# Routing of tokens inside an attention kernel: scratch in PSUM, larger groups, scatters at most three a tile, keys' sums on one engine

## The chip, the cores and the metric

The kernel runs on one core of one Trainium2 chip. The core has a matrix engine (TensorE, "PE" in the profile; its weight loads are shown apart as "PEld"), a vector engine (VectorE, "DVE"), a scalar engine (ScalarE, "ACT"), a general engine (GpSimd, "POOL") and the engine that issues most DMA transfers (SyncE, "SP"). SBUF is the on-chip memory of 128 partitions from which the engines read; PSUM is the small memory into which TensorE writes, in banks of 512 float32 for each partition. The metric is device time in microseconds (us) of one execution. A profile's "clock" is the TensorE clock that the throttle granted, as a share of full speed.

## The reference

Attention over pooled keys and values, then a layer of eight experts of which each token uses one, or none:

```python
# q, k, v: (8 batches, 8 heads, 576 positions, 64)
k_p = k.reshape(B, H, 72, 8, D).mean(axis=3)      # 72 pooled keys a head
v_p = v.reshape(B, H, 72, 8, D).mean(axis=3)
scores = scale * q @ k_p.transpose(0, 1, 3, 2)
attn = softmax(scores, axis=-1)                   # denominator + 1e-9
x = (attn @ v_p) as (4608 tokens, 512)

do_compute = x @ w_skip > 0
logits = x @ w_gate                               # 8 experts
e_idx = argmax(logits)
gate = softmax(logits)[e_idx]                     # denominator + 1e-9
out = x
out[do_compute] += gate * (relu(x @ w1[e_idx]) @ w2[e_idx])
```

## The kernel before

**Tiles.** The 4608 tokens are 36 tiles of 128 (`NT = 36`). A batch is four and a half tiles, so some tiles hold halves of two batches. A loop `for t in range(NT)` writes out a software pipeline by hand: in step t, PE computes the scores of tile t (`scores`, two halves), ACT the exponentials of tile t-1 (`exped`), PE the transposes of tile t-2 (`transposed`, `LAG` below is 4), PE the products with the values of tile t-4 (`values`, PSUM tile `o`), and DVE the division of tile t-5 (`normalised`: `rs` L353, `rc` L355, `l` L359, `x` L360, then the transfer of `x` to `out`). There is one `o`, so the products of a tile wait until DVE has read the tile before (L360). DVE also takes the largest score (`nm`, L302), whose result ACT needs. Sums of keys are done in `pool_k`: eight neighbours are added, for batches from 2 on as four additions of halves on POOL (L205, operand `stage`) and then four reductions of four on DVE (L208).

**Values.** `pool_v` adds the eight neighbours of a batch's values on POOL (L229 to L231, reading and writing `hlo`, `hhi` and `vl`; called the chain of a batch below), has PE and ACT work out their products with the skip and gate weights (`gs`), and writes the operand `vbd` of `values` on POOL (L272; the three buffers are vbd_121 to vbd_123 in the listings, used by batches b mod 3). Each output row of `values` thereby holds nine router numbers for each head beside the attention output.

**Routing.** `normalised` sums the nine router numbers over heads into `lg` in SBUF (L363). When a group of tiles is complete (`GROUPS`, here 6, 6, 6, 6, 6, 4 and 2 tiles), `route` is put on a queue of generators: it finds the largest logit (`r_mx`), which tokens skip (`r_no`, L379), the first expert that attains it (`r_eq`, `r_cm`, `r_oh`), by PE the rank of each token among those of its expert (`mps`, L399, read at L400 and L401), the place of the token's row in a table (`r_di`) and the gate (`r_se`, `pay`, L413). Then POOL issues one indirect DMA for each tile of the group (L415), which scatters the pairs of token and gate into `table` in DRAM. The function `extra` gives each step of t a budget (`BUDGET`) of these DVE instructions, after `nm` of the tile; a piece of keys' sums takes its share first, and one `w1lo` (the low part of a split weight, L538, on DVE) may follow. All instructions of one engine run in the order in which the program emits them.

**Early pair.** When the third group (tiles 0 to 17) is routed, `near_tokens` reads back the first expert's first 256 rows of the table (`nids`, L428, an SP transfer, which must wait for the scatters) and, `NWAIT = 3` steps of t later, gathers their rows of `out` by two indirect DMAs on POOL (L445).

**Order of the rest.** Weights of the first expert are loaded, rounded and split from tile 13 on (`w1hi`, `w1lo`, `w2hi`, `w2lo`; the low parts of w2 on POOL, L540). After tile 35 there is a tail until about 227 us, and then the experts' products, which keep PE busy to the end.

Of the kernel before, what the change touches and what calls it, by code (L numbers as in the profile page):

```python
# [26 lines left out]
F32 = mybir.dt.float32  # L27
F32R = mybir.dt.float32r
BF16 = mybir.dt.bfloat16
I32 = mybir.dt.int32  # L30
# [15 lines left out]
VA = HD + 10  # L46
GROUPS = [6, 6, 6, 6, 6, 4, 2]
EARLY = 18
# [12 lines left out]
WPOOL = 3  # L61
BUDGET = 7
DRAIN = 8
# [9 lines left out]
BIT = 3  # L73
NWAIT = 3
WARM = 3
# [83 lines left out]
def attention(tc, nc, q, k, vm, vr, cf, w1, w2, whi, wlo, out, c, pay, offs, table, load_constants, near, bufs, late, early, fin):  # L159
    with ExitStack() as ctx:  # L160
# [17 lines left out]
        for t in vl4:  # L178
            nc.gpsimd.memset(t[64:128], 0.0)
        lg = sp.tile([128, NT, 9], F32, name="lg")  # L180

# [10 lines left out]
        def pool_k(b, kt):  # L192

            kp_ = kp.tile([128, 4, SP], F32, name="kp")
            halves = [slice(hh * 64, hh * 64 + 64) for hh in range(2)]
            if b == 0:
                for g in range(4):
                    nc.vector.tensor_reduce(kp_[:, g], kt[:, g], axis=AX.X, op=ALU.add)
                    for hh, r in enumerate(halves):
                        nc.scalar.activation(kbd[0][r, g, hh * SP:(hh + 1) * SP], kp_[r, g], AF.Copy, scale=-SCALE)  # L200
                return
            n = POOL if b == 1 else 4
            if b > 1:
                for g in range(4):
                    nc.gpsimd.tensor_tensor(kt[:, g, :, 0:4], kt[:, g, :, 0:4], kt[:, g, :, 4:8], ALU.add)  # L205
            yield
            for g in range(4):
                nc.vector.tensor_reduce(kp_[:, g], kt[:, g, :, 0:n], axis=AX.X, op=ALU.add)  # L208
                yield
            for hh, r in enumerate(halves):  # L210
                nc.scalar.activation(kbd[b % 3][r, :, hh * SP:(hh + 1) * SP], kp_[r], AF.Copy, scale=-SCALE)
            yield
# [100 lines left out]
        def transposed(e):  # L313
# [7 lines left out]
            nc.scalar.activation(flat(pT), flat(pt), AF.Copy)  # L321
            pr = ps_p.tile([128, 4, 128], F32, name="pr")

            for a in range(2):
                nc.tensor.transpose(pr[:, a, :], part(a * 4 * SP + 128 - a * 2 * KL), ident)
            nc.scalar.activation(p4, pr[:, 0:2], AF.Copy)
            return pT, p4
# [16 lines left out]
        def normalised(t, os):  # L344
            x = ap.tile([128, H, HD], F32, name="x", bufs=3)
            l8 = ap.tile([128, H, 9], F32, name="l8")
            rs = ap.tile([128, 2, 4], F32, name="rs")
# [14 lines left out]
            yield  # L362
            nc.vector.tensor_reduce(lg[:, t, :], l8.rearrange("p h c -> p c h"), axis=AX.X, op=ALU.add)  # L363
            yield

        scatters = []

        def route(t0, n):

            l = lg[:, t0:t0 + n, 0:NE]  # L370
            skip = lg[:, t0:t0 + n, NE]
            bc = lambda x: x.unsqueeze(2).broadcast_to([128, n, NE])
            new = lambda name, *s, dt=F32: ap.tile([128, GMAX] + list(s), dt, name=name)[:, :n]
            mx = new("r_mx"); eq = new("r_eq", NE); cm = new("r_cm"); oh = new("r_oh", NE, dt=BF16); no = new("r_no")
            d = new("r_d", NE); ex = new("r_ex", NE); se = new("r_se")
            r8 = new("r_r8", NE); ds = new("r_ds"); di = new("r_di", dt=I32)
            nc.vector.tensor_reduce(mx, l, axis=AX.X, op=ALU.max)
            yield
            nc.vector.tensor_scalar(no, skip, 0.0, float(NO_TOKEN), ALU.is_le, ALU.mult)  # L379
            yield  # L380
            nc.vector.tensor_tensor(eq, l, bc(mx), ALU.is_equal)
            yield
            nc.vector.tensor_tensor(d, l, bc(mx), ALU.subtract)
            yield
            nc.vector.tensor_tensor(eq, eq, epos.unsqueeze(1).broadcast_to([128, n, NE]), ALU.mult)
            yield
            nc.vector.tensor_reduce(cm, eq, axis=AX.X, op=ALU.max)
            yield
            nc.vector.tensor_tensor(cm, cm, no, ALU.add)
            yield  # L390
            nc.vector.tensor_tensor(oh, eq, bc(cm), ALU.is_equal)
            yield NEXT
            nc.scalar.activation(ex, d, AF.Exp)

            pr = flat(ps_m.tile([128, 4, 128], F32, name="mps"))[:, 0:(n + 1) * NE].rearrange("p (j e) -> p j e", e=NE)
            for j in range(n):
                nc.tensor.matmul(pr[:, j:], c["ones"], oh[:, j].unsqueeze(1).broadcast_to([128, n + 1 - j, NE]),
                                 start=(j == 0), stop=False)
            nc.tensor.matmul(pr[:, 0:n], c["lower"], oh, start=False, stop=True)  # L399
            nc.vector.tensor_tensor(r8, pr[:, 0:n], offs.unsqueeze(1).broadcast_to([128, n, NE]), ALU.add)  # L400
            nc.vector.tensor_tensor(offs, offs, pr[:, n], ALU.add)  # L401
            yield NEXT
# [5 lines left out]
            yield  # L408
            nc.vector.tensor_scalar(se, se, 1e-9, None, ALU.add)
            yield  # L410
            nc.vector.tensor_tensor(di, ds, no, ALU.add)
            yield
            nc.vector.reciprocal(pay[:, t0:t0 + n, 1], se)  # L413
            for j in range(n):
                m = nc.gpsimd.indirect_dma_start(table, bass.IndirectOffsetOnAxis(ap=di[:, j:j + 1], axis=0),  # L415
                                                 pay[:, t0 + j, :], None, bounds_check=NE * NTOK - 1, oob_is_err=False)
                for other in scatters:
                    tc.declare_no_dep(m.ins, other, reason="rows of the table are written once")
                scatters.append(m.ins)
            if t0 + n == EARLY:  # L420
                yield from near_tokens()

        def near_tokens():
# [3 lines left out]
            nn = ap.tile([128, 1], F32, name="nn")  # L427
            nc.sync.dma_start(near["ids"], table[0:256].rearrange("(s l) t -> l s t", l=128))  # L428
            nc.vector.tensor_scalar(nn, count, 256.0, 2.0, ALU.is_ge, ALU.mult)
# [10 lines left out]
            nc.gpsimd.memset(bufs["ring"], 0.0)  # L440

            def gathers():
                nc.vector.tensor_scalar(near["slot"], near["ids"][:, :, 0], less, None, ALU.add)
                for i in range(2):
                    nc.gpsimd.indirect_dma_start(bufs["ring"][:, 3 + i, 0:D], None, out[0:EARLY * 128],  # L445
                                                 bass.IndirectOffsetOnAxis(ap=near["slot"][:, i:i + 1], axis=0),
                                                 bounds_check=EARLY * 128 - 1, oob_is_err=False)
            later[t + NWAIT] = gathers
            yield
# [145 lines left out]
        def extra(budget):  # L595

            if kcur in kg and t > max(0, 4.5 * kcur - KAHEAD):
                next(kg[kcur], None)
                if kcur == 1:
                    next(kg[kcur], None)  # L600
                budget -= 4
            while budget > 0 and routes.step():
# [4 lines left out]
        def add_routes(n):  # L607
            if n in ends:
                routes.gens.append(route(*ends[n]))

        def sums():
# [4 lines left out]
        for t in range(NT):  # L616
# [59 lines left out]
            if t >= WSTART:  # L676
                next(wgen, None)
            later.pop(t, lambda: None)()
            if t == NT - 4:
# [9 lines left out]
        for i, t in enumerate(range(NT - LAG, NT)):  # L689
# [8 lines left out]
            if i > 0:  # L698
                for _ in range(DRAIN):
                    routes.step(True)  # L700
            while los:
                los.pop(0)[1]()
# [33 lines left out]
        for _ in tail():  # L736
            side(STEP)
        for wait in slots(tc, nc, c, offs, table, near, bufs, out, fin, ap, ps_m):
            if wait:
# [509 lines left out]
```

## Time and profile before

| | before |
|---|---|
| time, median of 3 runs | 577.87 us (578.71, 575.75, 577.87) |
| profiled execution | 576.28 us, of which the span of instructions is 574.5 us |
| mean granted clock | 0.955 |
| attention, tiles 0 to 35 and tail | to about 227 us |
| experts | from there to 574.5 us |

The profile's page lists the busy time of each engine, the chain of work that ended last, and groups of instructions by line. In an entry "L360 x<-o,rc" the line is 360, the output `x` and the inputs `o` and `rc`. A timeline row gives start, duration, engine, line and operation, shape, and in brackets how long the engine had been idle and what released it. A busy time says little here: DVE is busy for half of the span, but PE waits for single instructions of it.

### The profile page before, as it was taken

What the parts mean: (1) busy time and instruction counts of PE and PEld (TensorE: products, weight loads), DVE (VectorE), ACT (ScalarE), POOL (GpSimd) and SP (SyncE); (2) the same over time, 40 slices, a digit from 0 to 9 for tenths busy, and PEclk for the clock granted to TensorE, in tenths of its full rate; (3) what the DMA queues carried; (4) which work ended last, traced back from release to release, by engine and by line L of the source; (5) the groups of instructions that cost most, each with busy time, mean ns of one, the idle gap of its engine ahead of it and who ended that gap; (6) DMA issues with size and microseconds to landing.
All of it is one profiled execution on the core that took longest, in us unless ns stands there. A gap on an engine that the chain in (4) does not pass through costs nothing. (4 is left out here: it accounts for less than half of the span.)

```text
span 574.5 us, 11135 instructions
## 1 busy us (share of the span) xinstructions
PE 518.3 (90%) x3347; PEld 464.5 (81%) x3348; DVE 315.4 (55%) x750; ACT 244.6 (43%) x672; POOL 234.5 (41%) x315
## 2 busy tenths in 40 slices
PE   7589979867499985899999999999999999999994
PEld 4389878767488964888889989989889888989893
DVE  3777886887566762224453535322363638465653
ACT  5458784847478101114142423112243436344441
POOL 4859496848843542311232123323242024304032
PEclk9679997978799998999999999999999999999998
DMA  8948897952579201111551235101144537572300
GB/s 296 395 182 311 299 200 254 262 215 102 204 221 234 96 2 39 48 39 41 200 173 41 81 143 184 63 29 52 55 138 153 188 130 248 191 255 68 124 26 8
DMA packets 33448, 86.05 MB, mean 150 GB/s; under 512 B 7485, under 2 KB 7746, under 8 KB 31488
## 3 DMA queue, kind: packets, MB, share of 16 engines
q1 hardware_dynamic: 25312, 71.62, 38.0%
q0 software_dynamic: 8096, 13.95, 7.4%
q8 instruction: 19, 0.31, 0.3%
q14 instruction: 21, 0.17, 0.1%
HBM read 73.79 MB, written 20.52 MB: 164 GB/s over the span
## 5 line engine op out<-in xcount | busy, mean ns | idle before, releaser
L1046 PE MATMUL psl<-xhi,w1hi 128*128 128x256 f32 (+3 forms) x416 | 122.1, 293 | 5.0 <-PEq L876 4.0
L1048 PE MATMUL psl<-xhi,w1lo 128*128 128x256 f32 (+3 forms) x416 | 121.3, 292 | 0.0
L1047 PE MATMUL psl<-xlo,w1hi 128*128 128x256 f32 (+3 forms) x416 | 121.3, 292 | 0.0
L965 POOL DMA_INDIRECT out<-ring,slot x39 | 39.5, 1013 | 180.2 <-POOLq L876 172.5
L1102 ACT ACTIVATE hhi<-psl 128x256 fp32r<-128x256 f32 (+4 forms) x104 | 41.9, 403 | 156.1 <-ACTq L876 155.1
L1061 PE MATMUL psf<-w2hi,hhi 128*128 128x512 f32 x240 | 96.1, 400 | 2.8 <-PEq L876 2.8
L1062 PE MATMUL psf<-w2lo,hhi 128*128 128x512 f32 x240 | 94.8, 395 | 0.0
L1159 DVE SCALAR_TENSOR_TENSOR hlo<-psl,hhi 128x256 fp32r<-128x256 f32 (+2 forms) x104 | 43.8, 423 | 79.2 <-DVEq L876 79.0
L1046 PEld LDWEIGHTS psl<-xhi,w1hi 128*128 128x128 f32 x416 | 78.1, 188 | 6.9 <-issue 6.3
L1064 PE MATMUL psf<-w2hi,hlo 128*128 128x512 f32 x200 | 79.1, 395 | 0.0
L1047 PEld LDWEIGHTS psl<-xlo,w1hi 128*128 128x128 f32 x416 | 78.2, 188 | 0.5
L1048 PEld LDWEIGHTS psl<-xhi,w1lo 128*128 128x128 f32 x416 | 78.1, 188 | 0.0
L339 PE MATMUL o<-vbd,pT 128*128 128x148 f32 (+1 forms) x304 | 53.8, 318 | 24.7 <-DVE x L360 20.3
L309 ACT ACTIVATE e<-sc,nm 128x72 f32<-128x72 f32 x288 | 64.6, 344 | 21.3 <-DVE nm L302 21.1
L339 PEld LDWEIGHTS o<-vbd,pT 128*128 128x128 f32 (+1 forms) x304 | 44.1, 194 | 27.6 <-issue 20.9
L1148 DVE SCALAR_TENSOR_TENSOR ring<-psf,ring 128x512 f32 x25 | 18.8, 750 | 79.0 <-DVEq L876 79.0
L1061 PEld LDWEIGHTS psf<-w2hi,hhi 128*128 128x128 f32 x240 | 45.1, 188 | 12.9 <-issue 3.2
L1062 PEld LDWEIGHTS psf<-w2lo,hhi 128*128 128x128 f32 x240 | 45.1, 188 | 9.7
L960 POOL DMA_INDIRECT ring<-out,slot x39 | 43.6, 1119 | 14.9 <-issue 12.5
L1111 ACT ACTIVATE xhi<-psd 128x512 fp32r<-128x512 f32 x36 | 18.9, 600 | 70.9 <-ACTq L876 70.9
L415 POOL DMA_INDIRECT table<-pay,r_di x36 | 36.4, 1010 | 30.9 <-DVE rc L355 11.5
L1064 PEld LDWEIGHTS psf<-w2hi,hlo 128*128 128x128 f32 x200 | 37.6, 188 | 9.1
(207 smaller groups left out, 914.6 us busy)
## 6 DMA issues: line engine op xcount, KB each, us to landing
stage<-in_w SPq DMA_DIRECT2D x64, 512.0 KB, 4.4
out<-x SPq DMA_DIRECT2D x36, 256.0 KB, 4.9
stage<-in_k SPq DMA_DIRECT2D x7, 1152.0 KB, 10.1
hlo<-in_vm SPq DMA_DIRECT2D x4, 1024.0 KB, 8.2
hhi<-in_vm SPq DMA_DIRECT2D x4, 1024.0 KB, 7.3
xlo<-in_q SPq DMA_DIRECT2D x6, 512.0 KB, 7.2
qt<-in_q SPq DMA_DIRECT2D x6, 512.0 KB, 5.6
xhi<-in_q SPq DMA_DIRECT2D x5, 512.0 KB, 7.6
```

The costliest lines, as they stand in the source:

```text
L309: nc.scalar.activation(e[:, h, :], sc[h // 4][:, h % 4 * SP:(h % 4 + 1) * SP], AF.Exp, bias=nm[:, h:h + 1], scale=-1.0)
L339: nc.tensor.matmul(o_[sl, g * 2 * VA:(g + 1) * 2 * VA], pT[:, 2 * a + g, sl], vbd[b % 3][:, 2 * a + g, :], start=(g == 0), stop=False)
L960: g.indirect_dma_start(ring[:, s % 6, 0:D], None, out, bass.IndirectOffsetOnAxis(ap=slot[:, s:s + 1], axis=0), bounds_check=NTOK - 1, oob_ ...
L965: g.indirect_dma_start(out, bass.IndirectOffsetOnAxis(ap=offsets, axis=0), ring[:, s % 6, 0:D], None, bounds_check=NTOK - 1, oob_is_err=Fa ...
L1046: t.matmul(ps, whi[0][:, k, w], xhi[:, k, xs], start=(k == 0), stop=False)
L1047: t.matmul(ps, whi[0][:, k, w], xlo[:, k, xs], start=False, stop=False)
L1048: last = t.matmul(ps, wlo[0][:, k, w], xhi[:, k, xs], start=False, stop=(k == 3))
L1061: t.matmul(ps, hhi[:, k, sl], whi[1][:, k, :], start=(k == 0), stop=False)
L1062: last = t.matmul(ps, hhi[:, k, sl], wlo[1][:, k, :], start=False, stop=(short and k == 7))
L1064: last = t.matmul(ps, hlo[:, k, sl], whi[1][:, k, :], start=False, stop=(k == 7))
L1102: a.activation(hhi[:, f, xs], psL[f % 3][:, xs], AF.Relu).then_inc(sem["act"], 1)
L1159: m = v.scalar_tensor_tensor(to[:, f], psL[f % 3][:, cs], 0.0, hhi[:, f, cs].bitcast(F32), ALU.max, ALU.subtract)
```

## The change

Five things are changed.

1. **Scratch in PSUM.** `lg` is gone. The router numbers `l8` of a whole group are kept in SBUF, and the first instruction of `route` reduces them over heads into a piece of PSUM, `scratch`, which is the unused second half of the bank of `pr`, one of the transposes' outputs. The comparisons, differences, ranks and sums of `route` are written there too, with new names in SBUF (`r_cn`, `r_sn`) where needed, so that each DVE instruction of `route` but the last group's has at most one operand in SBUF among its inputs. `r_eq` and its product with `epos` become one instruction (L392), and `r_d` takes the logits' own place. The last group uses a piece of SBUF instead.
2. **Groups** of 9, 9, 7, 6, 3 and 2 tiles, and a larger budget (10, of which a piece of keys' sums takes 7).
3. **Scatters** are not emitted with the gate but put on a list, of which each step of t emits at most three.
4. **Keys' sums** are on DVE alone, one reduction of eight for each of the four pieces.
5. **Early pair:** `nids` is emitted four steps after routing, and the gathers five steps after it.

```diff
-GROUPS = [6, 6, 6, 6, 6, 4, 2]
+GROUPS = [9, 9, 7, 6, 3, 2]
-BUDGET = 7
+BUDGET = 10
-NWAIT = 3
+SCATTERS = 3
+NIDS = 4
+NWAIT = 5
...
-        lg = sp.tile([128, NT, 9], F32, name="lg")
+        l8s = {}
+
+        side_ps = ps_p.tile([128, 4, 128], F32, name="pr")
+        pr, scratch = side_ps[:, 0:2], flat(side_ps)[:, 256:512]
...
-            n = POOL if b == 1 else 4
-            if b > 1:
-                for g in range(4):
-                    nc.gpsimd.tensor_tensor(kt[:, g, :, 0:4], kt[:, g, :, 0:4], kt[:, g, :, 4:8], ALU.add)
             yield
             for g in range(4):
-                nc.vector.tensor_reduce(kp_[:, g], kt[:, g, :, 0:n], axis=AX.X, op=ALU.add)
+                nc.vector.tensor_reduce(kp_[:, g], kt[:, g], axis=AX.X, op=ALU.add)
...
-            pr = ps_p.tile([128, 4, 128], F32, name="pr")
...
-            nc.vector.tensor_reduce(lg[:, t, :], l8.rearrange("p h c -> p c h"), axis=AX.X, op=ALU.add)
...
-            l = lg[:, t0:t0 + n, 0:NE]
-            skip = lg[:, t0:t0 + n, NE]
+            last = t0 + n == NT
+            m = n if last else GMAX
+            room = ap.tile([128, n * 20], F32, name="r_room", bufs=1) if last else scratch
+            lp = room[:, 0:n * 9].rearrange("p (j e) -> p j e", e=9)
+            l, skip = lp[:, :, 0:NE], lp[:, :, NE]
+            r8 = eq = room[:, m * 9:m * 9 + n * NE].rearrange("p (j e) -> p j e", e=NE)
+            cm, se, ds = (room[:, m * (17 + i):m * (17 + i) + n] for i in range(3))
...
+            nc.vector.tensor_reduce(lp, l8s.pop(t0)[:, :n].rearrange("p j h c -> p j c h"), axis=AX.X, op=ALU.add)
...
-            nc.vector.tensor_tensor(eq, l, bc(mx), ALU.is_equal)
-            yield
-            nc.vector.tensor_tensor(d, l, bc(mx), ALU.subtract)
-            yield
-            nc.vector.tensor_tensor(eq, eq, epos.unsqueeze(1).broadcast_to([128, n, NE]), ALU.mult)
+            nc.vector.tensor_tensor(l, l, bc(mx), ALU.subtract)
+            yield
+            nc.vector.scalar_tensor_tensor(eq, l, 0.0, epos.unsqueeze(1).broadcast_to([128, n, NE]), ALU.is_equal, ALU.mult)
...
-            for j in range(n):
+
+            def scatter(j):
                 m = nc.gpsimd.indirect_dma_start(table, ...)
...
+            pending.extend(lambda j=j: scatter(j) for j in range(n))
...
-            nc.sync.dma_start(near["ids"], table[0:256].rearrange("(s l) t -> l s t", l=128))
...
+            def ids():
+                assert not pending
+                nc.sync.dma_start(near["ids"], table[0:256].rearrange("(s l) t -> l s t", l=128))
...
+            later[t + NIDS] = ids
             later[t + NWAIT] = gathers
...
-                budget -= 4
+                budget -= 7
...
         def add_routes(n):
             if n in ends:
+                assert not routes.gens
                 routes.gens.append(route(*ends[n]))
+                next(routes.gens[0])
...
+            for _ in range(min(SCATTERS, len(pending))):
+                pending.pop(0)()
             later.pop(t, lambda: None)()
```

On DVE, at tile 22, the routing of the third group began before the change in the middle of the attention's own work:

```order
L302 TENSOR_REDUCE nm<-sc 128x4 x2
L363 TENSOR_REDUCE lg<-l_1545 128x9
L208 TENSOR_REDUCE kp<-stage 128x72
L377 TENSOR_REDUCE r_mx<-lg 128x6
L379 TENSOR_SCALAR r_no<-lg 128x6
L381 TENSOR_TENSOR r_eq<-lg,r_mx 128x48
L353 TENSOR_SCALAR rs<-o 128x8
L383 TENSOR_TENSOR r_d<-lg,r_mx 128x48
L355 RECIPROCAL rc<-rs 128x8
L385 TENSOR_TENSOR r_eq<-r_eq,cfs 128x48
L359 TENSOR_TENSOR l_1612<-o,rc 128x72
L360 TENSOR_TENSOR x<-o,rc 128x512
```

At the same tile it is now the second group, of nine tiles. In this listing `pr` is the scratch in PSUM, and `cfs` holds the constants (`epos`):

```order
L303 TENSOR_REDUCE nm<-sc 128x4 x2
L384 TENSOR_REDUCE pr<-l_905 128x81
L209 TENSOR_REDUCE kp<-stage 128x72
L386 TENSOR_REDUCE r_mx<-pr 128x9
L388 TENSOR_SCALAR r_no<-pr 128x9
L390 TENSOR_TENSOR pr<-pr,r_mx 128x9x8
L356 TENSOR_SCALAR rs<-o 128x8
L392 SCALAR_TENSOR_TENSOR pr<-pr,cfs 128x72
L358 RECIPROCAL rc<-rs 128x8
L394 TENSOR_REDUCE pr<-pr 128x9
L362 TENSOR_TENSOR l_1484<-o,rc 128x72
L363 TENSOR_TENSOR x<-o,rc 128x512
```

The instructions with two inputs in SBUF (`lg` with `r_mx`, `r_eq` with `cfs`) stand here with one input in PSUM, and the reduction over heads, once in each tile, is one for the group; every line of the changed kernel stands a little lower in the file. On POOL, before the change, the six scatters of the third group are followed by the values' chain (`hhi`), the gathers of the early pair (`ring<-out`), and the operand `vbd_121` that batch 6 uses:

```order
L415 DMA table<-pay,r_di 36864x2 x6
L540 TENSOR_TENSOR w2lo<-stage,w2hi 128x512 x2
L229 TENSOR_TENSOR hhi<-hhi 128x256 x4
...
L459 MEMSET hhi 128x8x128
L540 TENSOR_TENSOR w2lo<-stage,w2hi 128x512
L236 TENSOR_TENSOR vl_125<-ls,cfs 64x4x64
L540 TENSOR_TENSOR w2lo<-stage,w2hi 128x512
L445 DMA ring<-out,nslot 128x512 x2
L272 TENSOR_TENSOR vbd_121<-gs,cfs 128x8x9
L275 TENSOR_TENSOR vl_124<-gs,cfs 64x4x9
```

After the change it is nine scatters of the second group, ahead of the same chain:

```order
L423 DMA table<-pay,r_di 36864x2 x6
L554 TENSOR_TENSOR w2lo<-stage,w2hi 128x512
L423 DMA table<-pay,r_di 36864x2 x3
L554 TENSOR_TENSOR w2lo<-stage,w2hi 128x512
L230 TENSOR_TENSOR hhi<-hhi 128x256 x4
...
L473 MEMSET hhi 128x8x128
L554 TENSOR_TENSOR w2lo<-stage,w2hi 128x512
L237 TENSOR_TENSOR vl_125<-ls,cfs 64x4x64
L554 TENSOR_TENSOR w2lo<-stage,w2hi 128x512
L273 TENSOR_TENSOR vbd_121<-gs,cfs 128x8x9
L276 TENSOR_TENSOR vl_124<-gs,cfs 64x4x9
```

Three more scatters stand ahead of `vbd_121`, and the two gathers, which stood ahead of it, now come later. On SP, the transfer `nids` stood ahead of a load of weights and of the next outputs:

```order
L361 DMA out<-x 128x512 x2
L217 DMA hhi<-in_vm 128x2048
L218 DMA vl<-in_vr 64x512
L428 DMA nids<-table 128x2x2
L521 DMA stage<-in_w 128x2x512
L283 DMA xhi<-in_q 128x1024
L361 DMA out<-x 128x512 x2
```

Now it stands later, after the output of five more tiles:

```order
L364 DMA out<-x 128x512 x2
L535 DMA stage<-in_w 128x2x512
L284 DMA xlo<-in_q 128x1024
L364 DMA out<-x 128x512 x2
L284 DMA qt<-in_q 128x1024
L364 DMA out<-x 128x512
L453 DMA nids<-table 128x2x2
L544 DMA stage<-in_w 128x1024 x3
```

The weights, queries and five outputs (`out<-x`) that stood behind it no longer do.

## Prediction on record

> **What bounds the kernel now.** I read the windows first, then PE's timeline, and DVE's and POOL's at the places where PE stood.
>
> ```profile
> 35.00:57.50 22.50, 22.50 (x190) 21.59 (x190) 17.14 (x55) 18.69 (x72) 14.82 (x24) 1.00 0.69 246
> 82.00:92.70 10.70, 6.52 (x41) 5.59 (x41) 6.02 (x18) 3.67 (x14) 5.36 (x11) 0.68 0.97 210
> 93.00:107.40 14.40, 13.91 (x105) 12.61 (x104) 13.33 (x43) 12.99 (x46) 12.62 (x15) 1.00 0.82 270
> 112.90:123.50 10.60, 3.40 (x16) 3.38 (x16) 10.02 (x17) 2.75 (x12) 7.63 (x11) 0.68 0.63 222
> 133.00:140.40 7.40, 4.47 (x32) 4.01 (x32) 5.22 (x20) 3.88 (x13) 5.65 (x7) 0.77 0.13 40
> 148.30:160.90 12.60, 5.37 (x29) 5.25 (x29) 4.77 (x17) 2.66 (x12) 8.56 (x10) 0.59 0.77 291
> 161.00:176.20 15.20, 14.86 (x121) 13.55 (x120) 10.55 (x36) 14.31 (x53) 8.17 (x10) 1.00 0.71 199
> 300.00:574.00 274.00, 266.08 (x1614) 239.59 (x1612) 131.78 (x219) 94.12 (x158) 75.31 (x93) 0.99 0.35 116
> ```
>
> A window row gives its bounds and length, then the busy time of PE, PEld, DVE, ACT and POOL with their records, the granted clock, and the DMA share. From 300 us on PE is busy for 266 of 274 us, and the change leaves that alone. In the attention it is full in three quiet stretches (35, 93 and 161 us): 190 + 105 + 121 = 416 records in 52.1 us, 0.125 us a record at clock 1.00. In four others it stands, and then runs at a low clock: the 41 + 16 + 32 + 29 = 118 records there need 118 × 0.125 = 14.8 us by the quiet rate and took 10.70 + 10.60 + 7.40 + 12.60 = 41.3. **26.5 us** are lost there, which is the most that removing those stalls can bring. PE's timeline names what ended each:
>
> ```profile
> 84.17 0.69 PE L339 MATMUL o<-vbd,pT 128*64 128x148 f32 x4 [2.06 <-DVE x L360]
> 87.22 1.31 PE L339 MATMUL o<-vbd,pT 128*64 128x148 f32 x6 [2.12 <-POOL vbd L272]
> 120.15 1.32 PE L339 MATMUL o<-vbd,pT 128*128 128x148 f32 x4 [7.20 <-DVE x L360]
> 135.96 0.74 PE L339 MATMUL o<-vbd,pT 128*64 128x148 f32 x6 [2.93 <-DVE x L360]
> 155.59 1.32 PE L339 MATMUL o<-vbd,pT 128*128 128x148 f32 x4 [7.23 <-DVE x L360]
> ```
>
> The bracket is PE's idle time and its releaser. Four times it was L360, 0.68 us long itself; something sat ahead of it on DVE:
>
> ```profile
> 80.03 1.81 DVE L379 TENSOR_SCALAR r_no<-lg 128x6 f32<-128x6 f32 x1
> 111.07 7.75 DVE L381 TENSOR_TENSOR r_eq<-lg,r_mx 128x48 f32<-128x48 f32 x1
> 130.96 3.43 DVE L409 TENSOR_SCALAR r_se<-r_se 128x6 f32<-128x6 f32 x1
> 154.76 0.69 DVE L360 TENSOR_TENSOR x<-o,rc 128x512 f32<-128x512 f32 x1 [5.06 <-DMA out<-x]
> L381 DVE TENSOR_TENSOR r_eq<-lg,r_mx x7: 174/220/7755, 55.7 to 196.9; 128x48 f32<-128x48 f32 x5, 128x32 f32<-128x32 f32 x1, 128x16 f32<-128x16 f32 x1
> 108.77 3.05 POOL L205 TENSOR_TENSOR stage<-stage 128x288 f32<-128x288 f32 x4
> 118.31 0.44 POOL L230 TENSOR_TENSOR vl<-vl 64x128 f32<-64x128 f32 x1
> ```
>
> The median of L381 is 220 ns, and one took 7755: it began at 111.07 within POOL's L205 and ended at 118.8 with a POOL read of SBUF; the values' chain fills the time between. A DVE instruction with its inputs in SBUF was held here while POOL read SBUF back to back. I read L379 and L409, ten to twenty times their usual length for six elements, in the same way. The fifth row is another cause: x waited for a transfer, and SP's own waits say why:
>
> ```profile
> SPq L428 <- DMA table<-pay,r_di: 14.9, 1, 14.9
> ```
>
> SP stood for 14.9 us at `nids`, which waits for the scatters, and `out<-x` stood behind it.
>
> **The change part by part.**
>
> *Scratch in PSUM.* It rests on the contrast of one input in PSUM with two in SBUF:
>
> ```profile
> L360 DVE TENSOR_TENSOR x<-o,rc x34: 676/680/691, 35.4 to 195.8; 128x512 f32<-128x512 f32 x34
> L400 DVE TENSOR_TENSOR r_r<-mps,offs x7: 175/208/208, 61.6 to 199.8; 128x48 f32<-128x48 f32 x5, 128x32 f32<-128x32 f32 x1, 128x16 f32<-128x16 f32 x1
> L403 DVE TENSOR_TENSOR r_r<-r_r,r_oh x7: 168/201/1182, 65.3 to 200.1; 128x48 f32<-128x48 f32 x5, 128x32 f32<-128x32 f32 x1, 128x16 f32<-128x16 f32 x1
> ```
>
> L360 and L400 read PSUM and one SBUF operand: 34 and 7 instructions, none ever held (maxima 691 and 208 ns), and the scratch adds no more than 208 − 201 = 7 ns each. L403, two SBUF operands, reached 1182. So the holds of L379, L381 and L409 go. Removing POOL's L205 and the SP wait takes away the other two gaps (2.12 and 7.23) as far as nothing else is late. **−26.5**, everything late next being counted below.
>
> [...]
>
> *A smaller stall* at tile 4 ends in the same way:
>
> ```profile
> 29.55 1.79 DVE L272 TENSOR_TENSOR vbd<-gs,cfs 128x72 f32<-128x72 f32 x1 [1.48 <-ACT gs L266]
> 31.49 1.32 PE L339 MATMUL o<-vbd,pT 128*128 128x148 f32 x4 [2.23 <-DVE vbd L272]
> ```
>
> POOL then read for the first chain, which moves ahead as L205 before it goes. It can bring 0 to 2.2; I take **−1**.
>
> *Keys' sums and heads' sums.*
>
> ```profile
> L208 DVE TENSOR_REDUCE kp<-stage 128x72 f32<-128x288 f32 x24 | 10.6, 444 | 0.0
> L208 DVE TENSOR_REDUCE kp<-stage 128x72 f32<-128x576 f32 x4 | 2.8, 744 | 5.6 <-DMA stage<-in_k 5.6
> L363 DVE TENSOR_REDUCE lg<-l 128x9 f32<-128x72 f32 x36 | 9.8, 273 | 0.0
> DVE rs L353 <- PE o L341: 18.5, 21, 3.2
> ```
>
> DVE gains 24 × (744 − 444) = 7.2 us, spread over 24 tiles, and loses 36 × 273 = 9.8. The six group reductions come back: (744 − 444)/288 is 1.04 ns an element, so 2592 elements take 2.7 us and six starts of 0.14 make 3.6. DVE ends about 1 us better; in the tile of a reduction of nine (0.8 us) it is 0.5 to 0.8 worse. Its cover is DVE's wait for PE's `o`, 18.5 us in 21 waits, 0.9 each; where that is short, the reductions of tiles 13, 22 and 29 show. **+0.5**, between 0 and 1.8 (all three uncovered).
>
> *Scatters, gathers and `nids`.* POOL must do more ahead of batch 6's `vbd` (first used in tile 31) than before, as nine scatters in place of six stand there:
>
> ```profile
> 134.89 1.02 POOL L415 DMA_INDIRECT table<-pay,r_di  x1 [0.53 <-DVE less L431]
> 136.21 0.98 POOL L415 DMA_INDIRECT table<-pay,r_di  x1 [0.30 <-issue]
> 144.80 2.78 POOL L229 TENSOR_TENSOR hhi<-hhi 128x256 f32<-128x256 f32 x4
> 150.80 0.94 POOL L459 MEMSET hhi<- 128x1024 f32 x1
> 151.72 1.25 POOL L540 TENSOR_TENSOR w2lo<-stage,w2hi 128x512 fp32r<-128x512 f32 x1
> 152.94 0.60 POOL L236 TENSOR_TENSOR vl<-ls,cfs 64x256 f32<-64x256 f32 x1
> 165.59 0.68 DVE L360 TENSOR_TENSOR x<-o,rc 128x512 f32<-128x512 f32 x1
> ```
>
> From one scatter's start to the next is 1.3 us. Nine are 11.7, four w2lo at 1.25 are 5.0, the chain 150.80 − 144.80 = 6.0, the memset 0.94, L236 0.6: 24.2 us from the first scatter's start. The cap of three a tile is on their emission; on POOL nothing but w2lo stands between them. Tile 31's products could start in before at 166.3, when the L360 at 165.59 ended, 31.4 us after the first scatter at 134.89. Of these, the stretch at 148.3 lost 12.6 − 29 × 0.125 = 9.0, and that at 133, by what lay behind 134.89, about 2 more. So 20.4 us after its first scatter PE now wants `vbd`, and gets it 3.8 later. A gap of 2.93 lost 7.4 − 32 × 0.125 = 3.4 in the stretch at 133, the two gaps at 82 (4.18) lost 5.6: a gap costs its length and up to half more. **+5**, between 0 (if the gates come earlier) and 8. Batch 7's `vbd` has seven scatters ahead of it as well: **+0.5**. SP's wait at `nids` is now four tiles after routing, and runs beside that same wait.
>
> *w1lo* stays on DVE with two SBUF inputs, in tiles 18 to 23:
>
> ```profile
> L538 DVE TENSOR_TENSOR w1lo<-stage,w1hi x6: 658/684/734, 94.6 to 122.2; 128x512 fp32r<-128x512 f32 x6
> ```
>
> None was held before. With POOL's L205 and scatters moved, the values' chains of batches 5 and 6 run, by the order of emission, beside four of the six. A hold is 0 to 7.6 us; the common ones were 1.6 (L379, 1.81 − 0.2) and 1.0 (L403, 1.18 − 0.2). Two of four at 1.3, and a little for the clock behind: **+2.8**, between 0 and 9.
>
> *Transfers.* Once PE stands less, the same bytes come in less time. The DMA share was 0.97 at 82 us and 0.82 at full pace at 93, and one chain waited for its values:
>
> ```profile
> 92.64 3.23 POOL L229 TENSOR_TENSOR hhi<-hhi 128x256 f32<-128x256 f32 x4 [5.26 <-DMA hhi<-in_vm]
> ```
>
> Batches 5 and 6 could meet this with less slack. Bounds 0 and 5.3; I take **+1.5**.
>
> *Sum.* 576.3 (the profiled execution; the median stands 1.6 higher, the runs from 575.75 to 578.71) − 26.5 − 1 + 0.5 + 5 + 0.5 + 2.8 + 1.5 = **559**.
>
> **The rivals.**
>
> *B: nothing new is late.* The gates come early enough, no w1lo is held: 576.3 − 26.5 − 1 = 549. For it speaks that no w1lo was held; against it the 24.2 us of POOL work. 0.12.
>
> *C: the holds move to w1lo.* One of the six starts with a whole chain ahead of it, as L381 did. That costs its 7.2 gap and clock, 10.6 − 16 × 0.125 = 8.6, in place of the 2.8: 565; with a second of 3.4 or a late transfer, 571. 0.13.
>
> *D: the holds are not cured.* If POOL's reads hold any DVE instruction that takes an SBUF operand, the rows stay as they are and only the SP wait goes, which the late `vbd` returns: 575 to 579. The never-held L360 speaks against it. 0.05.
>
> *E: slower, by the shared bank.* The transposes' second output and the scratch now share one bank, and in that bank PE's transposes wait for DVE's scratch instruction, the scratch for ACT's copy, and the copy for PE, in some 12 tiles. Its price, if a handover stands in the open, is that of the one seen here:
>
> ```profile
> DVE r_r L400 <- PE mps L399: 4.7, 5, 1.4
> ```
>
> It is 4.7/5 = 0.94 us; three a tile in 12 tiles are 34 us, and 559 + 34 = 593. It turns the gain into a loss from (576 − 559)/12 = 1.4 us a routed tile. Against it: the scratch instructions come after a tile's `nm`, when ACT's copy of that tile should be over, and the next tile's transposes are half a tile away. 0.10. The Trainium skill (PSUM — Partial Sum Buffer, "PSUM bank collisions raise a hardware error") asks to guard by bank and not by address, so that two uses of halves of one bank must take turns; no run of before shows such a pair, and by that rule the handovers exist, whatever they cost.
>
> **How the numbers follow.** The sum 0.60, B 0.12, C 0.13, D 0.05, E 0.10. The range 546 to 573 runs from below B (with the early stall wholly gone) to C's upper end; D and E, 0.15, lie outside. About 0.5% (3 us) is what a measurement can tell from no change. Faster: 0.60 + 0.12 + 0.13 = 0.85; D is the same, 0.05; E slower, 0.10.
>
> **What would show it.** No routing instruction above 0.3 us and POOL without L205 show the cure. A PE gap of 2 to 5 us before `values` of tile 31, released by POOL's `vbd`, shows the late chain; without it, B. w1lo of over 1 us shows C. Waits of PE's `pr` for DVE, or of DVE's scratch for ACT, of a microsecond each, show E. SP's longest wait at `nids` should be under 5 us. I am wrong if the quiet rate of 0.125 us a record isn't reached between 80 and 160 us without any of these rows.

## The result, and the profile after

The changed kernel takes 561.88 us (median of 6 runs, 559.05 to 563.97) where before took 577.25 (6 runs): a ratio of 0.9733, 95% interval 0.9692 to 0.9773. The forecast was 559, from 546 to 573. The profiled execution took 559.05 us, 557.2 of it span, at a mean clock of 0.978 (before 0.955). The experts' first product stands in PE's timeline before, and after:

```profile
227.20 0.36 PE L1046 MATMUL psl<-xhi,w1hi 128*128 128x256 f32 x1 [3.13 <-PEq L876]
```

```profile
209.97 0.37 PE L1070 MATMUL psl<-xhi,w1hi 128*128 128x256 f32 x1 [3.11 <-PEq L900]
```

It comes 17.2 us earlier, which is the whole difference of the spans (17.3): nothing changed in the experts' stage. The windows of after, with the columns as in the prediction:

```profile
35.00:57.50 22.50, 22.50 (x190) 21.59 (x189) 15.96 (x44) 19.32 (x76) 13.78 (x22) 1.00 0.69 250
80.00:95.00 15.00, 15.00 (x131) 14.30 (x129) 12.36 (x34) 14.39 (x54) 12.25 (x13) 1.00 1.09 270
95.00:110.00 15.00, 9.40 (x63) 8.15 (x62) 6.50 (x14) 8.41 (x30) 6.98 (x13) 0.77 0.97 282
110.00:130.00 20.00, 18.05 (x158) 16.79 (x157) 16.65 (x57) 16.83 (x61) 14.49 (x18) 1.00 0.80 276
130.00:150.00 20.00, 15.41 (x126) 13.43 (x125) 12.39 (x38) 15.65 (x59) 18.89 (x24) 1.00 0.82 186
150.00:170.00 20.00, 18.50 (x155) 17.16 (x154) 14.50 (x46) 15.69 (x59) 11.93 (x13) 1.00 0.84 223
```

Only one stretch, 95 to 110 us, is still slow: clock 0.77, and 15 − 63 × 0.125 = 7.1 us lost. The idle time in the brackets of PE's rows between 60 and 170 us adds up to 23.1 us before and 14.8 after. That is 8.3 of the 17 us; the rest is rate, since four stretches at clocks of 0.59 to 0.77 have become one. What is left of the gaps, in PE's and DVE's timelines:

```profile
101.94 1.33 PE L339 MATMUL o<-vbd,pT 128*128 128x148 f32 x4 [5.59 <-DVE x L363]
111.37 0.41 PE L325 MATMUL pr<-cfs,e 128*128 128x128 f32 x2 [0.96 <-DVE l L362]
116.08 0.44 PE L325 MATMUL pr<-cfs,e 128*128 128x128 f32 x2 [0.99 <-DVE pr L407]
138.20 0.74 PE L339 MATMUL o<-vbd,pT 128*128 128x148 f32 x4 [2.70 <-DVE x L363]
148.93 0.74 PE L339 MATMUL o<-vbd,pT 128*128 128x148 f32 x4 [0.19 <-DVE x L363]
168.54 0.41 PE L325 MATMUL pr<-cfs,e 128*128 128x128 f32 x2 [1.31 <-DVE rs L356]
174.01 0.41 PE L325 MATMUL pr<-cfs,e 128*128 128x128 f32 x2 [1.39 <-DVE rs L356]
101.10 0.69 DVE L363 TENSOR_TENSOR x<-o,rc 128x512 f32<-128x512 f32 x1 [6.01 <-DMA out<-x]
137.36 0.69 DVE L363 TENSOR_TENSOR x<-o,rc 128x512 f32<-128x512 f32 x1 [3.38 <-DMA out<-x]
```

The two long gaps are no longer held instructions: DVE's L363 waits until a transfer of an older `x` has landed and its buffer is free. Around the first gap the transfers run at a share of about 1 (1.09 and 0.97 in the windows), around the second at 0.82. The first can be followed in DVE's row of the tile that used the same buffer before, in SP's, and in the summary of the 36 outputs (L364):

```profile
84.14 0.68 DVE L363 TENSOR_TENSOR x<-o,rc 128x512 f32<-128x512 f32 x1
84.85 3.80 SPq L364 DMA_DIRECT2D out<-x  x2
DMA to landing us min/median/max: 2.2/5.7/16.2
```

SP issued the output at 84.85 us, as soon as DVE had written `x`, and DVE's wait for it ended at 101.10, 16.2 us later, where the median output lands after 5.7. So the issue on SP was not late; the transfer behind it was. Seven short waits before `pr`, of 0.66 to 1.39 us (four are shown, 7.0 us in all seven), are handovers of the bank that the scratch shares: each ends when a DVE instruction on the scratch ends; the clock stayed at 1.00 around them. The routing's instructions themselves, by line (ns: least, median, most):

```profile
L392 DVE SCALAR_TENSOR_TENSOR pr<-pr,cfs x5: 191/224/242, 68.5 to 176.1; 128x72 f32<-128x72 f32 x2, 128x56 f32<-128x56 f32 x1, 128x48 f32<-128x48 f32 x1, 128x24 f32<-128x24 f32 x1
L398 DVE TENSOR_TENSOR r_oh<-pr,r_cn x5: 183/208/224, 71.2 to 176.8; 128x72 bf16<-128x72 f32 x2, 128x56 bf16<-128x56 f32 x1, 128x48 bf16<-128x48 f32 x1, 128x24 bf16<-128x24 f32 x1
L384 DVE TENSOR_REDUCE pr<-l x5: 540/1066/1337, 66.0 to 175.0; 128x81 f32<-128x648 f32 x2, 128x63 f32<-128x504 f32 x1, 128x54 f32<-128x432 f32 x1, 128x27 f32<-128x216 f32 x1
L552 DVE TENSOR_TENSOR w1lo<-stage,w1hi x6: 680/858/1209, 86.4 to 114.6; 128x512 fp32r<-128x512 f32 x6
```

L392, which now holds the comparison that had lasted 7.75 us, is 242 ns at most. Not every instruction that was held before had two inputs in SBUF: L379 (1.81 us) and L409 (3.43 us) are TENSOR_SCALARs with one. TENSOR_REDUCEs with one, like the sums over heads, never were. Shown are those sums before the change (L363), and from the changed kernel L388, which does the work of L379, and `nslot`, which still reads SBUF alone:

```profile
L363 DVE TENSOR_REDUCE lg<-l x36: 266/273/281, 36.8 to 196.4; 128x9 f32<-128x72 f32 x36
L388 DVE TENSOR_SCALAR r_no<-pr x5: 143/154/169, 68.0 to 175.7; 128x9 f32<-128x9 f32 x2, 128x7 f32<-128x7 f32 x1, 128x6 f32<-128x6 f32 x1, 128x3 f32<-128x3 f32 x1
L456 DVE TENSOR_SCALAR nslot<-nids,less x1: 1731/1731/1731, 149.4 to 149.4; 128x2 int32<-128x2 f32 x1
```

`nslot` took 222 ns before the change and 1731 after it. SP's own waits hold the read-back:

```profile
SPq L453 <- DMA table<-pay,r_di: 2.4, 1, 2.4
```

It stood for 14.9 us at `nids` before, and for 2.4 now.

### The profile page after: what moved, and what is told of

Read it like the earlier page. It is cut to its first block, busy times and chain, and to the rows that moved or that the text cites. A ratio compares the mean times of both kernels' runs of the same rounds, so it can differ in the third digit from the quotient of the medians.

```text
span 557.2 us, 11058 instructions
## 1 busy us (share of the span) xinstructions
PE 509.7 (91%) x3346; PEld 456.0 (82%) x3347; DVE 296.6 (53%) x698; ACT 244.7 (44%) x671; POOL 215.4 (39%) x291
## 5 line engine op out<-in xcount | busy, mean ns | idle before, releaser
L339 PE MATMUL o<-vbd,pT 128*128 128x148 f32 (+1 forms) x304 | 49.7, 300 | 9.8 <-DVE x L363 8.5
L339 PEld LDWEIGHTS o<-vbd,pT 128*128 128x128 f32 (+1 forms) x304 | 41.2, 184 | 11.7 <-issue 9.1
```

Source lines behind the costliest of these rows:

```text
L339: nc.tensor.matmul(o_[sl, g * 2 * VA:(g + 1) * 2 * VA], pT[:, 2 * a + g, sl], vbd[b % 3][:, 2 * a + g, :], start=(g == 0), stop=False)
```

## The experiments

The runs came in three sets of four. The kernels of one set ran on one chip beside runs of before, whose medians there were 573.82, 574.79 and 582.79 us, so ratios to before are compared and not times. The changed kernel itself was run again only on the third chip. Its ratio on the first two is not known, so the 0.9733 that the first two sets are held against comes from other runs, and the rows of the traces carry more of the argument than the ratios do. On the first two chips the traces show the same kinds of wait as the one above; on the third they do not.

### First set: scratch, shared bank, buffers of x

Four buffers for `x`:

```diff
-            x = ap.tile([128, H, HD], F32, name="x", bufs=3)
+            x = ap.tile([128, H, HD], F32, name="x", bufs=4)
```

> The changed kernel with four buffers for x in place of three (to make room, vs, ls, r_ex and r_oh have one buffer each). Theory: PE's two longest gaps after the change, 5.59 us before the values at 101.94 and 2.70 us at 138.20, are DVE's L363 waiting for the transfer of the x of three tiles before, which landed late while the transfers were at their full rate. One more buffer gives 3.6 us more, so the first gap falls to about 2 us, the second goes, and the time falls by 3 to 7 us, to about 556 to 559. Once they are gone, the operand vbd of batch 6, which POOL finished at 148.4 us, just as PE came for it, shows as a PE gap of up to 3 us. Rival: the transfers' rate itself is the bound between 80 and 105 us; then a gap of the same size shows at the next load (in_vm, in_q) and the time stays within 2 us of the changed kernel's 562.

Ratio 0.9738 (0.9689 to 0.9787), no better than 0.9733. The waits moved as the theory had it, in DVE's and PE's rows:

```profile
100.23 0.69 DVE L363 TENSOR_TENSOR x<-o,rc 128x512 f32<-128x512 f32 x1 [1.68 <-DMA out<-x]
142.47 1.35 PE L339 MATMUL o<-vbd,pT 128*128 128x148 f32 x4 [3.70 <-POOL vbd L273]
```

The wait for the transfer went from 6.01 to 1.68 us, the second one is gone, and PE then waited 3.70 us for batch 6's `vbd`. The profiled execution had a span of 553.5 us, 3.7 less than the changed kernel's, but the medians do not show a gain.

The transposes' second output in the bank of `mps`:

```diff
+            pr = ps_m.tile([128, 4, 128], F32, name="mps")[:, 0:2]
             for a in range(2):
                 nc.tensor.transpose(pr[:, a, :], part(a * 4 * SP + 128 - a * 2 * KL), ident)
```

> The changed kernel with the transposes' second output pr moved to the bank of mps, so that the routing's scratch has the bank to itself. Theory: seven PE waits of 0.66 to 1.39 us before pr (in sum about 7 us, with what the clock loses) are handovers of the shared bank, from DVE's scratch instruction to PE; they go, and the time falls by 4 to 8 us to about 555 to 558. Rival: mps has one buffer and its own readers (ACT's vT and gs, DVE's ranks), so pr waits for these instead, and the time stays within 3 us of 562 or rises.

Ratio 0.9927 (0.9889 to 0.9964): the rival was right. Other users of that bank now wait for ACT's copy of `pr`, PE's waits being:

```profile
PE mps L264 <- ACT p L327: 5.6, 7, 0.8
PE mps L255 <- ACT p L327: 5.3, 7, 0.9
```

These are 10.9 us where the handovers in the changed kernel were 7. The handovers moved to another bank, so what the time would be without any is not shown, and this way out of them is none.

The first part alone undone (with one buffer for `r_ex`, to make room):

```diff
-            room = ap.tile([128, n * 20], F32, name="r_room", bufs=1) if last else scratch
+            room = ap.tile([128, GMAX * 20], F32, name="r_room", bufs=1)
```

> The changed kernel with only the first part undone: the routing's scratch of every group lies in SBUF, and all the rest stays (groups, scatters, keys' sums on DVE, late read-back). Theory: the holds need two SBUF inputs on DVE beside POOL's reads; the values' chains at 63 to 70 and 107 to 117 us stand beside the first and second group's routing, so L390, L398 or L410 last 2 to 5 us again, and the time is 5 to 15 us above the changed kernel, 567 to 577. Rival: with the keys' sums gone from POOL little is left to hold DVE, and the shared bank's handovers go too, so that it is 553 to 560, faster than the changed kernel.

Ratio 0.9897 (0.9861 to 0.9933), 1.6 points worse than with the scratch in PSUM, as the theory said. The same lines with all their inputs in SBUF, two for L392 and L398 and one for L388:

```profile
L392 DVE SCALAR_TENSOR_TENSOR r_room<-r_room,cfs x6: 177/428/1864, 69.6 to 191.6; 128x72 f32<-128x72 f32 x2, 128x56 f32<-128x56 f32 x1, 128x48 f32<-128x48 f32 x1, 128x24 f32<-128x24 f32 x1
L398 DVE TENSOR_TENSOR r_oh<-r_room,r_cn x6: 165/216/4614, 72.7 to 192.7; 128x72 bf16<-128x72 f32 x2, 128x56 bf16<-128x56 f32 x1, 128x48 bf16<-128x48 f32 x1, 128x24 bf16<-128x24 f32 x1
L388 DVE TENSOR_SCALAR r_no<-r_room x6: 161/322/607, 68.6 to 191.3; 128x9 f32<-128x9 f32 x2, 128x7 f32<-128x7 f32 x1, 128x6 f32<-128x6 f32 x1, 128x3 f32<-128x3 f32 x1
```

Holds of up to 4.6 us are back, the long ones in the third group's routing and not, as expected, in the first two. This is one change against its undoing, and it shows that the holds come with the scratch in SBUF. It does not show that a second SBUF input is needed, since L388 has one and took up to 607 ns, against 169 with the scratch in PSUM. Nor is the whole loss of time the holds': PE's longest gap here is 9.02 us, of DVE's wait for a transfer of `x`, where it was 5.59 in the changed kernel.

The first part alone done: the changed kernel with the groups of 6, the budgets, the keys' sums on POOL, scatters and read-back at once, as before.

> The first part alone: the scratch in PSUM and the one reduction for a group, with the groups of 6, the budgets, the keys' sums on POOL, the scatters at once, the read-back at once and the gathers three tiles later, as before. Theory: the gaps by held routing instructions (2.06, 7.20 and 2.93 us) go, 14 us with their clock losses, the handovers of the shared bank cost about 5 back, and the gap of 7.23 us by the read-back's wait on SP stays, so 566 to 571. Rival: the holds move to w1lo, or the keys' sums on POOL cost as before: 572 to 578.

Ratio 0.9973 (0.993 to 1.0015): no change that can be told. That lies in the rival's range (572 to 578 us are 0.991 to 1.001 of 577.25), and one of its causes is seen, POOL's additions for the keys, but the largest loss is another. The holds were gone (none of its routing instructions on the scratch lasted over 0.22 us, the reductions over heads aside), but the time was not. Where it went, in PE's timeline, and then in the waits of SP, DVE and PE:

```profile
148.33 1.32 PE L343 MATMUL o<-vbd,pT 128*128 128x148 f32 x4 [10.26 <-DVE x L367]
```

```profile
SPq L443 <- DMA table<-pay,r_di: 15.2, 1, 15.2
DVE x L367 <- DMA out<-x: 11.3, 2, 10.9
PE o L343 <- POOL vbd L277: 5.6, 2, 3.4
```

PE's gap by SP's wait at the read-back (15.2 us, 14.9 before) grew from 7.23 to 10.26 us. I take it that PE has less of other stalls to hide that wait, which no run shows apart. POOL, with its additions for the keys, is late with `vbd` twice (5.6 us, 2.1 before). The holds' gain was given back to these waits, which the other parts are meant to remove.

### Second set: what the other parts are worth

No routing instruction between a tile's divisions:

```diff
             next(nrm, None)
-            routes.step()
             next(nrm, None)
-            routes.step()
             next(nrm, None)
```

> The changed kernel without the two routing instructions that were put between the divisions of a tile (rs, rc, x); routing goes on after nm only. Theory: PE's waits of 0.66 to 1.39 us before pr end with DVE instructions that stand between those divisions, since pr has to wait for the scratch instruction interleaved there; without them nothing in the shared bank is between one tile's nm and the next tile's pr, so these waits (7 us with the tail) go and the time falls by 3 to 7 us, a ratio to before of 0.960 to 0.968 where the changed kernel had 0.9733. Rival: the routing of a group takes a tile more, the scatters and batch 6's vbd come 3.6 us later and give it back: ratio 0.970 to 0.980.

Ratio 1.0023 (0.9973 to 1.0072), far above both expectations. The handovers inside the loop went (only those of the tail, 1.30 and 1.38 us, and two small ones are left), but routing took longer, and what hangs on it came late:

```profile
PE mps L486 <- DMA ring<-out,nslot: 6.6, 1, 6.6
PE o L339 <- POOL vbd L273: 4.4, 1, 4.4
PE o L339 <- DVE x L363: 7.6, 5, 4.6
```

The early pair's gather came 6.6 us after PE wanted it, `vbd` 4.4. The interleaving is worth more than the handovers cost.

Four buffers of `x`, and batch 6's `vbd` two tiles earlier:

```diff
-SUMS = [1, 2, 4]
+SUMS = [1, 2, 4, 4, 4, 4, 2, 4]
```

> Four buffers for x, as in the first of these experiments, and batch 6's vbd emitted two tiles earlier, so that POOL makes it after the first pieces of the next chain instead of behind the whole of it. Theory: with four buffers the gap that was left was 3.70 us, PE waiting for POOL's vbd behind the chain of batch 7; it goes, nothing else is late at that place, and the ratio to before is 0.962 to 0.970. Rival: another wait of the same tile takes its place (the read-back, the shared bank), and the ratio stays at 0.974.

Ratio 0.9738 (0.968 to 0.9797): the rival's figure. The 3.70 us gap for batch 6's `vbd` is gone. One of 1.36 us for batch 7's stands four tiles later, and DVE's `x` waited for its buffer again. PE's and DVE's rows:

```profile
165.86 0.77 PE L339 MATMUL o<-vbd,pT 128*64 128x148 f32 x6 [1.36 <-POOL vbd L273]
105.09 0.69 DVE L363 TENSOR_TENSOR x<-o,rc 128x512 f32<-128x512 f32 x1 [5.02 <-DMA out<-x]
```

With four buffers and the later `vbd` that wait was 1.68 us in the first set, at the same DMA share (1.03 from 80 to 105 us in both). Whether the chip, the order or the run makes the difference was not shown.

Scatters and read-back at once:

```diff
-            pending.extend(lambda j=j: scatter(j) for j in range(n))
+            for j in range(n):
+                scatter(j)
...
-            later[t + NIDS] = ids
```

with `nids` issued at the head of `near_tokens` and `NWAIT = 3`.

> The changed kernel with its scatters emitted at once, the early pair's rows read back at once and gathered three tiles later: the order of before, for groups of nine. Theory: SP stands at nids until the nine scatters have landed, some 13 us and more, out<-x and with it L363 of two or three tiles wait behind it, and PE stands for 5 to 11 us around tile 28: ratio 0.982 to 0.995. Rival: the transfers behind nids were late anyway, as PE waits for vbd there: ratio 0.973 to 0.978.

Ratio 0.9988 (0.9944 to 1.0032). Undoing the third and the fifth part together takes nearly the whole gain away. The gap, in PE's timeline, was in the range that the theory gave:

```profile
146.71 1.32 PE L339 MATMUL o<-vbd,pT 128*128 128x148 f32 x4 [10.38 <-DVE x L363]
```

The ratio is a little above its range.

The keys' first additions on POOL again:

```diff
+            n = POOL if b == 1 else 4
+            if b > 1:
+                for g in range(4):
+                    nc.gpsimd.tensor_tensor(kt[:, g, :, 0:4], kt[:, g, :, 0:4], kt[:, g, :, 4:8], ALU.add)
```

> The changed kernel with the first half of the keys' sums on POOL again (24 additions of 0.79 us, DVE's reductions 0.44 instead of 0.74 us). Theory: the additions stand ahead of values' chains and vbd on POOL, 3.1 us a batch, and hold w1lo; PE waits 2 to 4 us for vbd at two places, and the ratio is 0.978 to 0.988. Rival: DVE's 7 us are worth more than POOL's 19, and the ratio is 0.965 to 0.972.

Ratio 0.989 (0.9797 to 0.9983), just above the theory's range, from four runs; the interval covers most of that range. The mechanism was another: no gap ended with `vbd`. PE's longest, 7.98 us, was by the wait of `x` for its transfer, and the waits before `pr` came to 7.3 us, about as in the changed kernel.

### Third set: another chip

The changed kernel again:

> The changed kernel once more, unaltered, on the same chip as the other three of this call, so that they can be held against it. Every theory: a ratio to before of 0.969 to 0.977, as measured first.

Ratio 0.9923 (0.9885 to 0.9961), outside the range expected: less than a third of the gain first measured. On this chip something else stops the engines. POOL's scatters, DVE's, ACT's and PE's rows:

```profile
81.12 1.07 POOL L423 DMA_INDIRECT table<-pay,r_di  x1 [1.68 <-DVE rs L356]
91.50 0.98 POOL L423 DMA_INDIRECT table<-pay,r_di  x1 [0.30 <-issue]
83.91 0.41 PE L341 MATMUL o<-vl,p 128*64 128x148 f32 x2
93.56 0.17 DVE L356 TENSOR_SCALAR rs<-o 128x8 f32<-128x8 f32 x1 [10.70 <-remote]
94.43 0.60 ACT L322 ACTIVATE pT<-pt 128x512 f32<-128x512 f32 x1 [8.69 <-remote]
94.97 1.33 PE L339 MATMUL o<-vbd,pT 128*128 128x148 f32 x4 [8.81 <-DVE x L363]
```

PE's product for DVE's L356 ended at 84.3 us, and DVE began it at 93.56, "remote" meaning that nothing on the core shown released it just then. The nine scatters ran from 81.12 to 92.48. DVE and ACT stood until they were over; ACT stood again in the bursts at 163 and 191 us (4.1 and 10.2 us). In the changed kernel's first trace the same nine ran from 80.31 on, and PE was busy for 15.00 of 15.00 us (the window at 80). Why this chip's engines stop, and what before's trace looks like there, was not measured. It is left open.

Only 8 of 128 partitions of the first expert's weights:

```diff
-                    nc.sync.dma_start(chunk_view(st[cc], cc), chunk_src(w1, w2, 0, cc))
+                    nc.sync.dma_start(chunk_view(st[cc], cc)[0:8], chunk_src(w1, w2, 0, cc)[0:8])
```

> The changed kernel loading only 8 of 128 partitions of each piece of the first expert's weights during the attention (3.9 MB less; the rest of those weights is zero, so the first expert's results differ; POOL clears three stage buffers at the start). Theory: the wait of DVE's L363 for the transfer of an old x is the transfers' rate between 80 and 105 us, where their share is 1.03; with a quarter less to move the gaps of 5.59 and 2.70 us go, batch 6's vbd shows instead with 2 to 4 us, and the time falls by 3 to 7 us against the changed kernel. Rival: x waits for its place in SP's queue, not for the rate; then the gap stays at 4 to 6 us and so does the time.

Ratio 0.9958 (0.992 to 0.9997), the same as the changed kernel's on this chip. Neither trace shows a wait of `x` for a transfer, perhaps because the stops leave the transfers time, so it tells nothing of the two theories. The rows of the changed kernel's first trace say more: there the output was issued at once and took 16.2 us to land.

The groups of before:

```diff
-GROUPS = [9, 9, 7, 6, 3, 2]
+GROUPS = [6, 6, 6, 6, 6, 4, 2]
```

> The changed kernel with the groups of before, 6, 6, 6, 6, 6, 4 and 2, and all the rest as changed. Theory: the groups' size is worth little: one more group costs one or two more handovers of the shared bank (1 us each), three scatters fewer ahead of batch 6's vbd give nothing while the transfers are late there; within 3 us of the changed kernel, ratio 0.970 to 0.980. Rival: larger groups are a main part of the gain; then 6 us or more slower, ratio above 0.983.

Ratio 0.9782 (0.9696 to 0.9867), where the groups of nine had 0.9923 (0.9885 to 0.9961) on this chip: the intervals do not overlap, so smaller groups are better there by about 1.4 points, though from only four runs. No difference over 3 us was expected. That fits stops as long as a burst of scatters. In its trace, which is of the slowest of the four runs, the longest such wait of DVE in the loop ended just after a burst of six (99.25 to 106.7 us):

```profile
108.00 0.46 DVE L303 TENSOR_REDUCE nm<-sc 128x4 f32<-128x288 f32 x1 [3.15 <-remote]
```

That is 3.15 us against 10.70 for nine. What the groups are worth on the first chips was not tried.

Four buffers, the earlier `vbd` and later weights:

```diff
-WSTART = 13
+WSTART = 16
```

> A version meant to beat the changed kernel: four buffers for x, batch 6's vbd two tiles earlier, and the first expert's weights loaded from tile 16 on instead of 13. Theory: the transfers' rate at 80 to 105 us is the bound that is left, and three tiles' worth of weights (0.75 MB) move out of it to 150 us and later, where it has room; the x gap falls to under 2 us, no vbd gap appears, and the time is 4 to 9 us under the changed kernel, ratio 0.957 to 0.966. Rival: the weights, or the early pair's products that need them, come late at tile 34 and PE waits there instead: ratio 0.970 to 0.980.

Ratio 0.9882 (0.9821 to 0.9944), an interval that overlaps the changed kernel's there, and above both ranges expected; a gain cannot be told behind the stops. Apart from the groups of six on this chip, no version that was run beats the changed kernel clearly.

## Why the prediction was right, point by point

**The 26.5 us of stalls.** Right in cause, with one reading too narrow: the contrast was drawn between one input in PSUM and two in SBUF, but L379 and L409 were held with a single input in SBUF. The cure covers them all the same, as they now read PSUM. None of the four places is a held routing instruction now, undoing the scratch brings holds of 1.9 and 4.6 us back, and undoing the later read-back brings a gap of 10.4. But the parts are not a sum: the scratch alone brought 0.3%, which cannot be told from nothing, and SP's and `vbd`'s waits were longer in its trace.

**Batch 6's `vbd`, +5.** Its mechanism was right, its effect hidden. From POOL's timeline after the change:

```profile
124.53 1.02 POOL L423 DMA_INDIRECT table<-pay,r_di  x1 [0.16 <-DVE x L363]
148.16 0.30 POOL L273 TENSOR_TENSOR vbd<-gs,cfs 128x72 f32<-128x72 f32 x1
```

From first scatter to `vbd` took 23.6 us (24.2 forecast), and PE came for it at 148.9, since the gap of 2.70 us and handovers had made PE late itself. With that gap removed by a fourth buffer, PE waited 3.70 us (3.8 forecast). In the changed kernel the term is zero.

**Transfers, +1.5.** The step that was mis-sized. I took the nearest row, a load that waited 5.26 us, and asked only for loads. What came late were the outputs: three buffers of `x` cover 3 tiles, and the two gaps are 8.3 us, beyond the upper bound of 5.3. The landing of 16.2 us, with an issue that was not late, puts the first of them down to the transfers.

**The shared bank, in the sum as nothing.** Rival E's wait exists at its price (0.66 to 1.39 us against 0.94), but seven times and not 36: 7 us. My reason against it, that scratch stands only after `nm`, was wrong, since `route` also steps between the divisions, ahead of the next `pr`. Five of the seven waits (4.3 us) come so. The other two (2.7 us) are in the tail, and stayed at 1.30 and 1.38 us when nothing stood between the divisions. So a term of 7 us was left out, and it stood in for the `vbd` that cost nothing. That the time came within 3 us of 559 is therefore partly luck: errors cancelled.

**The signs.** The sign of B held, no gap for `vbd`, without B's time. That of C showed too, one w1lo of 1.21 us, without C's price, and that of E seven times, at a fifth of its price. The quiet rate was not reached between 95 and 110 us, and the wait behind that, `x` for its output, was none of the rows that the signs name.

**Smaller terms.** w1lo lasted 1.3 us longer in all (2.8 forecast, the longest 1209 ns). A reduction of nine over heads took 1.34 us, not 0.8. The early stall fell from 2.23 to 1.34 us (0.9, forecast 1).

## What to carry to other kernels

In these traces a DVE instruction fed from SBUF alone, a TENSOR_TENSOR with two inputs or a TENSOR_SCALAR with one, could be held through a row of POOL instructions that read SBUF (7.75 us). With one input in PSUM the routing's lines took at most 242 ns, the sums over heads aside. So that is a cure, but in a pipeline with one output buffer it pays only when the next wait in the same place goes too. Before summing removed stalls, ask for each queue what it will be late with once they are gone, outputs waiting for a buffer included. A cap on instructions emitted in a step is no cap on an in-order queue's burst.

## What was not expected of the hardware

On one of three chips, DVE and ACT stood for up to 10.7 us while POOL issued nine indirect scatters back to back, in waits whose producer had long ended; the two other sets show no such wait. The gain of this change was 2.7% on the chip first measured and 0.8% there. Four buffers of `x` met a wait of 1.68 us in one set and, with the earlier `vbd`, 5.02 in another, at the same DMA share of 1.03.
